# Retention, then a softplus and a squared-ReLU layer: the first chunks' loads on two queues, and three idle products ahead instead of six

## The chip, the cores and the metric

The kernel runs on one core of a Trainium2 chip. The metric is the device time of one execution in microseconds (us); the median of three timed runs stands for the kernel before. The engines are PE (TensorE, matrix products), DVE (VectorE), ACT (ScalarE), POOL (GpSimd) and SP (SyncE, which here only issues DMAs). ACT can issue DMAs too: such an instruction stands in ACT's own instruction stream, between its arithmetic.

## What is computed

A retention layer (attention with a decay in place of the softmax) of 4 sequences, 8 heads, 576 positions and 64 dimensions, and behind it two feed-forward layers over its 2304 x 512 result. All is float32.

```python
scores = scale * np.matmul(q, k.transpose(0, 1, 3, 2))
Dmat = np.where(rel >= 0, gamma[:, None, None] ** rel[None, :, :], 0.0)
attn = np.matmul(scores * Dmat, v)
x = attn.transpose(0, 2, 1, 3).reshape(2304, 512)
h = x @ w_in;   x = (np.maximum(h, 0) + np.log1p(np.exp(-np.abs(h)))) @ w_out
h = x @ w2_in;  out = np.square(np.maximum(h, 0)) @ w2_out
```

## The kernel before

The 2304 tokens are worked off in tiles of 512 and 384 tokens. The retention goes chunk by chunk (128 tokens, 8 heads, a running state), most of it woven into the steps of the first feed-forward layer. Only the four chunks of the first tile have nothing to be woven into: they are worked off ahead of everything else, in an order that is written out by hand (`with tc.manual_schedule()`), in which each engine's instructions stand in the order of the calls. This head of the program is the first 30 us, and the change is in it alone.

For each of the four chunks there are two loads. `early_qk` (L982 to L989) brings q and k with the dimensions on the partitions: four heads lie on partitions 0 to 63 (`LO`) and four on 64 to 127 (`HI`), 256 KB each, by one DMA for each half. `early_kv` (L991 to L994) brings k and v with the tokens on the partitions, 512 KB by one DMA. All of these are issued by SP, in the order of the chunks, and behind them, also by SP, the first three weight tiles (`wi_raw`, `pump_load(3)`, 512 KB each, L132) and the q, k and v of the fifth chunk (`ring`, L359). ACT issues four small loads: the table `cst` in two halves and two rows `rows_in`.

A layer below the kernel gives each DMA one of eight semaphores in turn. A DMA that takes a semaphore over waits, on the engine that issues it, until the DMA that had the semaphore before has landed. So no more than eight DMAs are under way, and which DMA waits for which follows from the order in which SP and ACT together issue them.

The engines' part of a chunk: PE makes the scores `pb` (`early_scores`, L1006), DVE multiplies them with the causal mask (`early_mask`, L1027) and v with its weights (`early_v`, L1015), PE adds to the state `st` (L1038), ACT copies it (L1044), PE makes the output `po` (L1054, L1062), DVE scales it to `x` (L1076), ACT rounds x to its upper part `xh` (L1081), and DVE makes the lower part `xl` (L1091). The scale tables in `cst` are not loaded whole: PE spreads the two rows over the partitions (`spread_rows`, L1135), ACT copies the result (L1139, L1140) and makes some of the tables by 20 small operations (L1145), DVE the others (L963). Behind the third chunk ACT begins on the first weight tile: L152 and L153 put its two words in shape, DVE joins them (L157), ACT rounds (L185), DVE takes the rest (L186), and PE can begin the first layer (`early_g1`, L1110).

Ahead of all this PE multiplies zeros (`keep_warm(6)`, L946), six products of 128 x 512 into a bank that nobody reads; one more such product stands behind `spread_rows`.

Of the kernel before, what the change touches and what calls it, by code (L numbers as in the profile page):

```python
# [45 lines left out]
def kernel(  # L46
# [26 lines left out]
    nc = tc.nc  # L73
# [203 lines left out]
    def pump_load(upto):  # L277
        while n_load[0] < min(upto, len(loads)):
            load_w(*loads[n_load[0]])
            n_load[0] += 1  # L280
# [68 lines left out]
    LO, HI = slice(0, P // 2), slice(P // 2, P)  # L349
# [5 lines left out]
    def load_chunk(c):  # L355
        if c < NPR:
            new_chunk(c)
            for i, src in ((0, qk_t), (2, kv)):
                nc.sync.dma_start(  # L359
                    out=chunk[c][:, i:i + 2],  # L360
                    in_=src[2 * c:2 * c + 2].rearrange("s p i h c -> (s p) i h c"),
                )
# [580 lines left out]
    def keep_warm(count, n=512):  # L943

        for _ in range(count):
            nc.tensor.matmul(  # L946
                cold[:, :n], lhsT=warm[:, :P], rhs=warm[:, :n], start=True, stop=True
            )
# [11 lines left out]
    def make_xw(m, n):  # L960


        nc.vector.scalar_tensor_tensor(  # L963
            out=later[:, m - 1:m - 1 + n],
            in0=cst[:, x_first].rearrange("p (a b) -> p a b", a=KD).unsqueeze(1)
            .to_broadcast([P, n, KD, CN]),
            scalar=1.0,
            in1=times[:, m - 1:m - 1 + n].unsqueeze(3).to_broadcast([P, n, KD, CN]),
            op0=ALU.mult, op1=ALU.mult,
        )  # L970
# [4 lines left out]
    qks, kvs, mixed, kept_s, pbs, pos, xs_of, kept_of = {}, {}, {}, {}, {}, {}, {}, []  # L975
    causal = first_pool.tile([P, P], F32, tag="causal", name="causal", bufs=1)

    def early_tiles(c):
        qks[c] = first_pool.tile([P, 2, 2, HH, CN], F32, tag=f"qk{c}", name="qk", bufs=1)
        kvs[c] = first_pool.tile([P, 2, H, CN], F32, tag=f"kv{c}", name="kv", bufs=1)  # L980

    def early_qk(c):  # L982
        for g, half in enumerate((LO, HI)):
            nc.sync.dma_start(
                out=qks[c][half].rearrange("p i s h c -> p i s (h c)"),
                in_=qk_t[2 * c:2 * c + 2].rearrange("s p i h c -> p i s (h c)")[
                    ..., g * HH * CN:(g + 1) * HH * CN
                ],
            )  # L989

    def early_kv(c):  # L991
        nc.sync.dma_start(
            out=kvs[c], in_=kv[2 * c:2 * c + 2].rearrange("s p i h c -> (s p) i h c")
        )  # L994

    def early_scores(c):
        if c % 2:
            pb = pbs[c] = [ps_h.tile([P, 512], F32, tag=f"h{g}", name="pb") for g in range(2)]
        else:
            pb = ps_head.tile([P, 2, 512], F32, tag="pb", name="pb", bufs=1)  # L1000
            pbs[c] = [pb]
            pb = [pb[:, g] for g in range(2)]
        for hh in range(HH):
            for s, to in enumerate((LO, HI)):
                for g, rows in enumerate((LO, HI)):
                    nc.tensor.matmul(  # L1006
                        pb[g][to, hh * P:(hh + 1) * P],
                        lhsT=qks[c][rows, 1, s, hh, :], rhs=qks[c][rows, 0, :, hh, :],
                        start=True, stop=True, skip_group_check=True,
                    )  # L1010

    def early_v(c):
        t = kvs[c][:, 1]
        w = vw[:, 2 * c * H:(2 * c + 1) * H]
        nc.vector.tensor_tensor(  # L1015
            out=t, in0=t, in1=w.unsqueeze(2).to_broadcast([P, H, D]), op=ALU.mult
        )

    def early_mask(c):
        mixed[c] = first_pool.tile([P, H, P], F32, tag="mixed", name="mixed")  # L1020
        for g, pb in enumerate(pbs[c]):
            n = H // len(pbs[c])
            if len(pbs[c]) == 1:
                pb = pb.rearrange("p g (h n) -> p (g h) n", n=P)
            else:
                pb = pb.rearrange("p (h n) -> p h n", n=P)
            nc.vector.tensor_tensor(  # L1027
                out=mixed[c][:, g * n:(g + 1) * n], in0=pb,
                in1=causal.unsqueeze(1).to_broadcast([P, n, P]), op=ALU.mult,
            )  # L1030
# [59 lines left out]
    def early_low(c):  # L1090
        nc.vector.tensor_tensor(  # L1091
            out=early_at(x_lo(), c), in0=xs_of.pop(c), in1=early_at(x_hi(), c),
            op=ALU.subtract,
        )
# [31 lines left out]
    def spread_rows():  # L1126
        rows = ps_head.tile([P, 2, 512], F32, tag="po", name="rows", bufs=1)
        to = [
            rows[:, 0, at:at + n * b].rearrange("p (a b) -> p a b", a=n)
            for at, n, b in ((0, KD, CN), (256, SCN - 1, KD))  # L1130
        ]
        for half in (LO, HI):
            one = slice(half.start, half.start + 1)
            for r, of in zip(to, (row[0][:, 0], row[0][:, 1:, :, 0])):
                nc.tensor.matmul(  # L1135
                    r[half], lhsT=ones[one], rhs=of[one],
                    start=r is to[0], stop=True, skip_group_check=True,
                )
        nc.scalar.copy(cst[:, x_first].rearrange("p (a b) -> p a b", a=KD), to[0])  # L1139
        nc.scalar.mul(times, to[1], float(D) ** 0.5)  # L1140

    def scalar_xw(m, n):
        for m in range(m, m + n):
            for a in range(KD):
                nc.scalar.activation(  # L1145
                    out=later[:, m - 1, a], in_=cst[:, C_XW + a * CN:C_XW + (a + 1) * CN],
                    func=AF.Copy, scale=times[:, m - 1, a:a + 1],
                )

    with tc.manual_schedule():  # L1150
        rows_in = xs.tile([P, SCN * KD * CN], F32, tag="xr", name="rows_in")
        for c in range(last):
            early_tiles(c)
        early_qk(0)
        for half in (LO, HI):
            nc.scalar.dma_start(out=cst[half, :C_XW], in_=consts[CN:P, :C_XW])
        early_kv(0)
        early_qk(1)
        early_kv(1)
        for r in (0, CN):  # L1160
            nc.scalar.dma_start(out=rows_in[r:r + 1], in_=consts[r:r + 1, C_XW:])
        nc.scalar.preload_act_table_set("natural_log_exp_and_others")
        for c in range(2, last):
            early_qk(c)
            early_kv(c)
        pump_load(3)
        load_chunk(last)
        nc.vector.memset(causal[LO, CN:], 1.0)
        nc.vector.memset(causal[HI, :CN], 0.0)

        for half, to, of, n in ((LO, 0, 0, SCN), (HI, 0, 1, SCN - 1), (HI, SCN - 1, 0, 1)):
            nc.vector.tensor_copy(
                vw[half, to * H:(to + n) * H], cst[half, C_VW + of * H:C_VW + (of + n) * H]
            )
        for s, half in enumerate((LO, HI)):
            nc.vector.tensor_copy(
                causal[half, s * CN:(s + 1) * CN], cst[half, C_MASK:C_MASK + CN]
            )
        keep_warm(6)
        early_scores(0)  # L1180
        row.append(rows_in.rearrange("p (m a b) -> p m a b", a=KD, b=CN))
        spread_rows()
        keep_warm(1)
        scalar_xw(4, 2)
        early_mask(0)
        early_v(0)
        make_xw(1, 1)
        early_scores(1)
        early_states(0)
        early_mask(1)  # L1190
        early_v(1)
        early_carried(0)
        early_o(0)
        early_x(0)
        early_scores(2)
        early_states(1)
        scalar_xw(6, 1)
        early_carried(1)
        early_o(1)
        make_xw(2, 2)  # L1200
        early_mask(2)
        early_v(2)
        early_x(1)
        scalar_xw(7, 2)
        early_scores(3)
        early_states(2)
        early_carried(2)
        early_o(2)
        early_low(0)
        early_mask(3)  # L1210
        early_v(3)
        begin_words()
        early_keep(0)
        early_x(2)
        next(begun[0])
        early_low(1)
        early_keep(1)
        early_states(3)
        early_carried(3)
        early_o(3)  # L1220
        next(begun[0])
        begun.clear()
        begin_words()
        early_g1(0)
        early_x(3)
        next_state(3, 1)
        begin_words()
        early_low(2)
        early_low(3)
        early_keep(2)  # L1230
        for made in begun:
            next(made)
        early_keep(3)
# [232 lines left out]
```

## Time and profile before

| | us |
|---|---|
| median of three runs | 840.74 (837.81 to 841.48) |
| span of the profiled execution | 839.0 |
| PE busy | 818.2 (98%) |
| DVE busy | 702.2 (84%) |
| ACT busy | 475.3 (57%) |
| DMA queues, mean rate | 226 GB/s |

The profiled execution's span, from its first to its last instruction, is 1.7 us below the median. PE is busy nearly throughout, so the time is the sum of PE's work and of what PE waits for. Shares over the whole span say nothing of the head, whose limits are others; for it one reads the rows in order of time. In these rows a line that issues DMAs is marked SPq or ACTq: the start is when the engine began to issue, the time what the issuing took, not the transfer. A row of several instructions shows its group's start and the whole stretch.

### The profile page before, as it was taken

The page shows a single profiled execution, that of the slowest core. Times are in us where ns is not written, and L with a number is a line of the kernel's source. Part 1 is how long each engine was busy: PE and PEld are TensorE (multiplying, and loading weights), DVE is VectorE, ACT ScalarE, POOL GpSimd, SP SyncE. Part 2 cuts the span into 40 slices and gives each one's busy share as a digit, 9 for nine tenths or more (in the row PEclk, how much of TensorE's full clock was granted, in tenths as well). Part 3 has the DMA queues.
Part 4 walks back from the last instruction along what each step waited for, and adds up shares of the span by engine and source line. Part 5 has one row for each costly group of instructions (what it writes and reads, how often), then busy time and mean ns, then how long its engine had stood idle before and what let it go on. Part 6 is the DMA issues. An engine that isn't in the chain of part 4 may idle for free.

```text
span 839.0 us, 16498 instructions
## 1 busy us (share of the span) xinstructions
PE 818.2 (98%) x5957; PEld 722.6 (86%) x5957; DVE 702.2 (84%) x1336; ACT 475.3 (57%) x899; POOL 0.2 (0%) x4
## 2 busy tenths in 40 slices
PE   8899999999999998999999999999999999999998
PEld 5677799888788876888799999988999988999887
DVE  4889887878988887787999988999698997787886
ACT  3889888757567667676888521355321554111453
POOL 0000000000000000000000000000000000000000
PEclk9999999999999999999999999999999999999999
DMA  9866544546656665466676688898988889988885
GB/s 234 298 195 235 167 141 145 176 152 214 210 174 198 224 190 176 149 227 202 210 255 219 221 253 249 259 296 275 301 257 245 255 263 280 284 254 252 254 268 176
DMA packets 122804, 189.39 MB, mean 226 GB/s; under 512 B 10466, under 2 KB 68450, under 8 KB 122722
## 3 DMA queue, kind: packets, MB, share of 16 engines
q1 hardware_dynamic: 122560, 188.26, 71.3%
q8 instruction: 47, 0.77, 0.4%
q14 instruction: 33, 0.27, 0.1%
q10 hardware_dynamic: 164, 0.09, 0.1%
HBM read 147.41 MB, written 40.89 MB: 224 GB/s over the span
## 4 chain that ended last, share of the span: by engine, by line
PE 78%; DVE 8%; ACT 8%; DMA 3%; issue 2%; SPq 0%; DVEq 0%; ACTq 0%
PE acc L563 17%; PE ph L512 16%; PE py L699 9%; PE py L772 9%; PE px L699 6%; PE pz L772 6%; PE px L772 6%; PE pz L699 6%; ACT l L527 1%; DMA wi_raw<-in_moe_w_in_dram 1%; DVE l L535 1%; DVE e L532 1%; ACT e L526 1%; ACT e L525 1%; PE po L436 1%
## 5 line engine op out<-in xcount | busy, mean ns | idle before, releaser
L512 PE MATMUL ph<-xh,wi 128*128 128x512 f32 (+1 forms) x632 | 145.1, 371 | 2.2 <-ACT l L527 1.1
L512 PEld LDWEIGHTS ph<-xh,wi 128*128 128x128 f32 x632 | 116.3, 189 | 18.7 <-issue 1.4
L563 PE MATMUL acc<-gl,woh 128*128 128x512 f32 (+1 forms) x320 | 119.0, 372 | 2.9 <-DVE gl L548 2.9
L563 PE MATMUL acc<-gh,woh 128*128 128x512 f32 (+1 forms) x320 | 120.5, 380 | 0.5 <-ACT woh L185 0.5
L563 PE MATMUL acc<-gh,wol 128*128 128x512 f32 (+1 forms) x320 | 118.7, 371 | 0.7 <-DVE wol L186 0.7
L532 DVE SCALAR_TENSOR_TENSOR e<-e 128x512 f32<-128x512 f32 (+1 forms) x80 | 51.0, 638 | 48.7 <-ACT l L527 47.8
L699 PE MATMUL py<-t,sring 128*128 128x384 f32 x432 | 88.6, 339 | 0.0
L525 ACT ACTIVATE e<-ph 128x512 f32<-128x512 f32 (+1 forms) x80 | 44.2, 553 | 60.9 <-PE ph L512 60.4
L512 PE MATMUL ph<-xl,wi 128*128 128x512 f32 (+1 forms) x316 | 77.9, 367 | 0.1
L699 PEld LDWEIGHTS py<-t,sring 128*128 128x128 f32 x432 | 74.8, 188 | 2.6 <-DVE uring L903 0.7
L563 PEld LDWEIGHTS acc<-gl,woh 128*128 128x128 f32 x320 | 60.4, 189 | 12.1 <-DVE gl L548 5.1
L752 ACT CAST gh<-g 128x384 fp32r<-128x384 f32 x84 | 43.1, 515 | 46.6 <-PE px L772 16.7
L563 PEld LDWEIGHTS acc<-gh,woh 128*128 128x128 f32 x320 | 60.4, 189 | 9.8 <-ACT woh L185 0.8
L563 PEld LDWEIGHTS acc<-gh,wol 128*128 128x128 f32 x320 | 60.5, 189 | 8.7 <-DVE wol L186 1.0
L752 ACT CAST gring<-g 128x384 fp32r<-128x384 f32 x84 | 43.1, 514 | 40.3 <-PE py L772 16.4
L512 PEld LDWEIGHTS ph<-xl,wi 128*128 128x128 f32 x316 | 58.1, 188 | 8.0 <-DVE xl L479 0.4
L899 ACT COPY uring<-px 128x384 f32<-128x384 f32 x24 | 11.5, 481 | 87.5 <-PE px L699 87.5
L699 PE MATMUL pz<-t,sring 128*128 128x384 f32 x288 | 58.4, 334 | 0.0
L699 PE MATMUL px<-t,sring 128*128 128x384 f32 x288 | 58.0, 335 | 0.0
L527 ACT ACTIVATE l<-e,cst 128x512 f32<-128x512 f32 (+1 forms) x80 | 54.4, 681 | 5.8 <-DMA x2d<-xo 3.6
L720 DVE TENSOR_TENSOR gring<-g,gring 128x384 fp32r<-128x384 f32 x84 | 46.2, 553 | 10.0 <-ACT gring L752 8.9
L720 DVE TENSOR_TENSOR gl<-g,gh 128x384 fp32r<-128x384 f32 x84 | 46.4, 554 | 9.2 <-ACT gh L752 8.0
(126 smaller groups left out, 1622.3 us busy)
## 6 DMA issues: line engine op xcount, KB each, us to landing
sring<-s2d SPq DMA_DIRECT2D x168, 256.0 KB, 3.2
sring<-o2d SPq DMA_DIRECT2D x168, 256.0 KB, 3.4
wi_raw<-in_moe_w_in_dram SPq DMA_DIRECT2D x32, 512.0 KB, 5.0
wo_raw<-in_moe_w_out_dram SPq DMA_DIRECT2D x32, 512.0 KB, 4.1
s2d<-ct SPq DMA_DIRECT2D x48, 256.0 KB, 2.7
o2d<-ct SPq DMA_DIRECT2D x48, 256.0 KB, 2.6
ring<-in_qk_t_dram SPq DMA_DIRECT2D x14, 512.0 KB, 4.8
ring<-in_kv_dram SPq DMA_DIRECT2D x14, 512.0 KB, 6.1
```

The costliest lines, as they stand in the source:

```text
L436: nc.tensor.matmul(po[(LO, HI)[hh % 2], hh // 2, :], lhsT=before[rows, hh, :] if carried else sv[:, hh, :], rhs=qp[:, hh, :] if carried el ...
L512: nc.tensor.matmul(ph[:, :n], lhsT=a, rhs=x, start=(j == 0), stop=(j == len(todo) - 1))
L525: nc.scalar.activation(out=e, in_=ph[:, :n], func=AF.Abs)
L526: nc.scalar.activation(out=e, in_=e, func=AF.Exp, scale=-1.0)
L527: nc.scalar.activation(out=l, in_=e, func=AF.Ln, bias=below_one, scale=1.0 + 2.0**-23)
L532: nc.vector.scalar_tensor_tensor(out=e, in0=e, scalar=-2.0, in1=e, op0=ALU.add, op1=ALU.mult)
L563: nc.tensor.matmul(acc[j][:, :n], lhsT=a, rhs=x, start=(begin and m == 0), stop=(end and m == 2))
L699: nc.tensor.matmul(ps, lhsT=a, rhs=x, start=(first and m == 0), stop=(m == len(todo) - 1), skip_group_check=True,)
L720: nc.vector.tensor_tensor(out=out, in0=a, in1=b, op=ALU.subtract)
L752: nc.scalar.copy(h, src)
L772: nc.tensor.matmul(blocks[m][:, :cols], lhsT=a[:, c], rhs=x, start=(first and p == n == 0), stop=(p == NP - 1 and n == len(todo) - 1), ski ...
L899: nc.scalar.copy(s1, px)
```

## The change

`early_qk` issues the lower half by SP as before and the upper half by ACT. `early_kv` issues k by SP and v by ACT, 256 KB each, where one DMA of 512 KB stood. `keep_warm(6)` becomes `keep_warm(3)`. Nothing else differs, and the orders of PE, DVE and POOL are the same but for the three products; line numbers behind L994 go up by two.

```diff
     def early_qk(c):
-        for g, half in enumerate((LO, HI)):
-            nc.sync.dma_start(
+        for g, (half, queue) in enumerate(((LO, nc.sync), (HI, nc.scalar))):
+            queue.dma_start(
                 out=qks[c][half].rearrange("p i s h c -> p i s (h c)"),
...
     def early_kv(c):
-        nc.sync.dma_start(
-            out=kvs[c], in_=kv[2 * c:2 * c + 2].rearrange("s p i h c -> (s p) i h c")
-        )
+        for i, queue in enumerate((nc.sync, nc.scalar)):
+            queue.dma_start(
+                out=kvs[c][:, i],
+                in_=kv[2 * c:2 * c + 2, :, i].rearrange("s p h c -> (s p) h c"),
+            )
...
-        keep_warm(6)
+        keep_warm(3)
         early_scores(0)
```

The first place is ACT's stream from its first instruction on. Before, four small DMAs, the load of the activation tables, and then the copy of the spread rows (DMAHW is one of the eight semaphores of DMAs; a row without brackets waits for nothing):

```order
L1156 DMA cst<-in_consts_dram 64x138 x2
L1161 DMA rows_in<-in_consts_dram 1x2304 x2
L1162 ACT_TABLE_LOAD
L1139 COPY cst<-rows 128x256 [waits PE_49]
L1140 ACTIVATE times<-rows 128x32
```

Of the change, from ACT's second instruction on:

```order
L1158 DMA cst<-in_consts_dram 64x138 x2
L993 DMA kv<-in_kv_dram 128x512
L984 DMA qk<-in_qk_t_dram 64x4x256
L993 DMA kv<-in_kv_dram 128x512 [waits DMAHW2_49]
L1163 DMA rows_in<-in_consts_dram 1x2304 [waits DMAHW3_49]
L1163 DMA rows_in<-in_consts_dram 1x2304 [waits DMAHW7_49]
L1164 ACT_TABLE_LOAD
L984 DMA qk<-in_qk_t_dram 64x4x256 [waits DMAHW3_49]
L993 DMA kv<-in_kv_dram 128x512 [waits DMAHW5_49]
L984 DMA qk<-in_qk_t_dram 64x4x256 [waits DMAHW7_49]
L993 DMA kv<-in_kv_dram 128x512 [waits DMAHW0_49]
L1141 COPY cst<-rows 128x256 [waits PE_49]
```

Eight large DMAs now stand in ACT's stream (the first of them, the upper q and k of chunk 0, just ahead of these rows), seven of ACT's DMAs have a wait, and the copy of the spread rows stands behind all of them. By the built program the last one, v of chunk 3, waits until semaphore 0 has counted three DMAs: the upper q and k of chunk 0, k of chunk 1, and the first weight tile.

The second place is the same stream at ACT's first work on that weight tile. Before:

```order
L1145 ACTIVATE cst<-cst,times 128x64 x8
L1044 COPY kept<-st 128x256 [waits PE_49,Activation_49]
L152 ACTIVATE wi_raw<-wi_raw 128x512 [waits DMAHW0_49]
L153 ACTIVATE wi_raw<-wi_raw,cst 128x512 [waits DMAHW2_49]
L1081 CAST xh<-x 128x4x128 [waits DVE_49]
```

Of the change:

```order
L1147 ACTIVATE cst<-cst,times 128x64 x8
L1046 COPY kept<-st 128x256 [waits PE_49,Activation_49]
L152 ACTIVATE wi_raw<-wi_raw 128x512
L153 ACTIVATE wi_raw<-wi_raw,cst 128x512 [waits DMAHW4_49]
L1083 CAST xh<-x 128x4x128 [waits DVE_49]
```

L152 has lost its wait for the weight tile's DMA: that wait now stands further up in ACT's stream, at the DMA of v of chunk 3.

The third place is SP's stream up to the weight tiles. Before, from the second half of chunk 2's q and k on:

```order
L984 DMA qk<-in_qk_t_dram 64x4x256 [waits DMAHW3_49]
L992 DMA kv<-in_kv_dram 128x1024 [waits DMAHW4_49]
L984 DMA qk<-in_qk_t_dram 64x4x256 [waits DMAHW5_49]
L984 DMA qk<-in_qk_t_dram 64x4x256 [waits DMAHW6_49]
L992 DMA kv<-in_kv_dram 128x1024 [waits DMAHW7_49]
L132 DMA wi_raw<-in_moe_w_in_dram 128x4x256 [waits DMAHW0_49]
```

Of the change, from k of chunk 1 on:

```order
L993 DMA kv<-in_kv_dram 128x512 [waits DMAHW0_49]
L984 DMA qk<-in_qk_t_dram 64x4x256 [waits DMAHW1_49]
L993 DMA kv<-in_kv_dram 128x512 [waits DMAHW4_49]
L984 DMA qk<-in_qk_t_dram 64x4x256 [waits DMAHW5_49]
L993 DMA kv<-in_kv_dram 128x512 [waits DMAHW6_49]
L132 DMA wi_raw<-in_moe_w_in_dram 128x4x256 [waits DMAHW0_49]
```

On SP eight DMAs of 256 KB stand ahead of the first weight tile where it was twelve of 256 and 512 KB; that tile's DMA waits for k of chunk 1, where it waited for the upper q and k of chunk 1.

## Rows read from the trace of the kernel before

**Rows 1.** The page's first line.
```profile
span 839.0 us, 16498 instructions
```

**Rows 2.** Chain of waits, head: start, time, what.
```profile
11.28 11.36 DMA wi_raw<-in_moe_w_in_dram
```

**Rows 3.** Timeline of ACT: start, stretch, instructions, idle time ahead and its cause.
```profile
1.97 1.03 ACTq L1161 DMA_DIRECT2D rows_in<-in_consts_dram  x2
3.03 1.28 ACT L1162 ACT_TABLE_LOAD   x1 [3.03 <-issue]
10.81 0.37 ACT L1139 COPY cst<-rows 128x256 f32<-128x256 f32 x1 [6.50 <-PE rows L1135]
11.32 2.02 ACT L1145 ACTIVATE cst<-cst,times 128x64 f32<-128x64 f32 x8
13.51 0.37 ACT L1044 COPY kept<-st 128x256 f32<-128x256 f32 x1 [0.17 <-PE st L1038]
15.42 0.62 ACT L1081 CAST xh<-x 128x512 fp32r<-128x512 f32 x1 [1.54 <-DVE x L1076]
17.39 1.06 ACT L1145 ACTIVATE cst<-cst,times 128x64 f32<-128x64 f32 x4
22.66 0.68 ACT L152 ACTIVATE wi_raw<-wi_raw 128x512 f32<-128x512 f32 x1 [0.40 <-DMA wi_raw<-in_moe_w_in_dram]
```

**Rows 4.** Windows: busy time by engine, granted clock (1.00 is full), DMA share, GB/s.
```profile
0.00:2.90 2.90, 1.45 (x2) 0.84 (x3) 0.74 (x4) 0.00 (x0) 0.20 (x4) 1.00 0.25 19
2.90:11.26 8.36, 8.36 (x53) 3.80 (x51) 1.98 (x6) 1.73 (x3) 0.00 (x0) 1.00 1.08 265
11.26:15.34 4.08, 3.44 (x68) 2.37 (x66) 3.47 (x8) 2.42 (x10) 0.00 (x0) 1.00 1.10 255
15.34:19.27 3.93, 3.70 (x81) 2.87 (x81) 2.99 (x5) 1.95 (x6) 0.00 (x0) 1.00 1.09 253
19.27:22.64 3.37, 3.03 (x72) 2.38 (x74) 2.42 (x5) 2.80 (x10) 0.00 (x0) 1.00 1.09 353
33.00:36.40 3.40, 3.40 (x10) 2.70 (x9) 3.19 (x6) 1.15 (x2) 0.00 (x0) 0.52 1.02 404
```

**Rows 5.** Timeline of DVE, same columns as the timeline of ACT.
```profile
11.87 0.42 DVE L963 SCALAR_TENSOR_TENSOR cst<-cst,times 128x256 f32<-128x256 f32 x1
12.90 1.29 DVE L1027 TENSOR_TENSOR mixed<-pb,causal 128x512 f32<-128x512 f32 x2 [0.61 <-PE pb L1006]
14.10 0.68 DVE L1015 TENSOR_TENSOR kv<-kv,vw 128x512 f32<-128x512 f32 x1
14.70 0.68 DVE L1076 TENSOR_TENSOR x<-po,cst 128x512 f32<-128x512 f32 x1
15.30 0.68 DVE L963 SCALAR_TENSOR_TENSOR cst<-cst,times 128x512 f32<-128x512 f32 x1
16.52 1.23 DVE L1027 TENSOR_TENSOR mixed<-pb,causal 128x1024 f32<-128x1024 f32 x1 [0.54 <-PE pb L1006]
```

**Rows 6.** Who waited for whom on SP's queue, first 30 us: total, times, longest.
```profile
SPq L132 <- DMA kv<-in_kv_dram: 1.4, 1, 1.4
```

**Rows 7.** Timeline of PE, same columns.
```profile
1.45 7.58 PE L946 MATMUL cold<-warm 128*128 128x512 f32 x12 [1.45 <-DVE warm L940]
32.38 0.68 PE L388 MATMUL pb<-ring 64*64 64x64 f32 x16 [2.65 <-DVE ring L398]
32.99 3.67 PE L512 MATMUL ph<-xh,wi 128*128 128x512 f32 x8
39.76 2.09 PE L512 MATMUL ph<-xh,wi 128*128 128x512 f32 x8 [1.07 <-ACT l L527]
```

## The prediction

> **What bounds the kernel now.** Over the whole span PE is at work for 98% of 839.0 us [rows 1], so anything that shifts the head of the program shifts the end; nothing later is tied to the clock on the wall. The chain of waits says what sets the head: the first weight tile is issued at 11.28 and lands 11.36 later, at 22.64 [rows 2], and ACT's first operation on it, L152, starts at 22.66 after an idle time of 0.40 for that DMA [rows 3]. That is the number to watch: from L152 on, ACT and DVE hand the weight tiles to one another with no other wait for a load, and PE's first layer follows. Next read the timeline of ACT: it waits 6.50 for the spread rows, starts its copy at 10.81, and has from there to 22.66, 11.85 us, for its part of the first chunks [rows 3]. So two things must be ready for L152: the tile, and ACT itself. ACT is ready only 0.40 before the tile; it has no more slack than that. Third, the windows: from 2.9 to 19.27 the queues move 265, 255 and 253 GB/s, then 353 [rows 4]. The edges 11.26, 15.34 and 19.27 are about where the upper q and k of chunks 1, 2 and 3 land, so each of the second and third windows holds one chunk, 1.05 MB in 4 us. The slow windows hold the loads that fill only 64 partitions each; the fast one holds loads over all 128.
>
> **The change part by part.**
>
> *The halves at once.* What the split can bring is the rate. At 353 GB/s a chunk would take 3.0 us instead of 4.0, about 4 us over four chunks. The first tile then lands earlier; by how much comes next.
>
> *When the first weight tile lands.* Ahead of it on SP's queue are eight pieces of 262,144 bytes, 2.10 MB, and itself 0.52: 2.62 MB. On ACT's queue, moved beside them, are the upper halves and v of chunks 0 and 1 (1.05 MB), the tables (0.09) and the upper q and k of chunk 2 (0.26), 1.40 MB, and at most 0.5 of the later pieces, which wait for others. I take 4.1 MB in all, with the two queues sharing alike (an estimate; before, ACT's queue held next to nothing). Before, the windows give 5.49 MB moved by 22.64 [rows 4], while q, k, v, the tables and the tile are 4.80; so a landing is seen some 0.69/0.353 = 2.0 us after its last byte. With a start at 2.7 (2.9 less what had moved by then) the tile lands at 2.7 + 4.1/0.353 + 2.0 = 16.3 at the fast rate and at 2.7 + 4.1/0.26 + 2.0 = 20.5 at the slow one. I take the middle, 18.4: halves run side by side only while both queues have work, and ACT's runs dry whenever its next issue waits.
>
> *ACT's stream.* This is the cost. A DMA that waits holds back everything behind it on its engine: SP shows it, its weight-tile issue waited 1.4 us for a kv load [rows 6]. ACT now has eight large DMAs ahead of its first copy, and the last, v of chunk 3, waits for semaphore 0, that is for the first weight tile to have landed. L152 has even lost its own wait for it. So ACT's copy, at 10.81 before, starts at 18.4 plus that last issue, 0.5 (half of the 1.03 for two [rows 3]): 18.9. Queued behind it: the copy of the spread rows, all of ACT's table operations, the copies of the state, the casts. Waiting for these: DVE's L963 and with it the mask of chunk 1, and PE's first output, whose bank the spread rows still hold.
>
> *How long ACT then needs to L152.* All loads but the last v's have landed or land before their turn, so DVE's waits of 0.61 and 0.54 for scores [rows 5] and most of ACT's 1.54 for x [rows 3] go. Counted from ACT's copy: at 0.5 the rows are spread (11.32 - 10.81 [rows 3]); DVE does table, masks, v and x of chunk 0, 0.42 + 1.29 + 0.68 + 0.68, with some 0.08 of overlap at each seam (14.10 against 12.90 + 1.29 [rows 5]), to 3.4; then tables, mask 1.23, v and x of chunk 1, 0.68 three times, to 6.3. ACT's own work up to there, 2.02 + 0.37 + 0.62 + 0.37 + 1.06 [rows 3], is 4.4 and hidden. Behind x of chunk 1 ACT casts (0.62), makes eight tables (2.02), copies the state (0.37): 9.3. Before it was 11.85, so the waits for loads that go are worth 2.5 us. L152 starts at 18.9 + 9.3 = 28.2 instead of 22.66: **5.5 us later**. With 9.3 to go, ACT's copy would have to start by 22.66 - 9.3 = 13.4 for nothing to change.
>
> *Three idle products fewer.* The six take 7.58 us as twelve passes and end at 9.03 [rows 7]; three end near 6, and the scores of chunk 0 can start once q and k are there. That gains nothing: PE's next work needs `rows_in`, which ACT issued at 1.97 before [rows 3] and now issues only after the upper q and k of chunk 1 have landed. PE is idle there for some 5 us. [...] Here PE mostly waits for DVE, so the price lies between 0 and 1.6; I take 0.4, nearer to the cover. It cannot be below nothing, since fewer products make PE no warmer. ACT's table load (1.28 [rows 3]) lies in the idle time.
>
> *The sum.* 5.5 + 0.4 = 5.9 us. The span would go from 839.0 to 844.9, and the median, which lies 1.7 above the span, from 840.74 to **846.6**. The bounds: the tile at 16.3 gives 3.4, the tile at 20.5 gives 7.6 and with 1.6 for the clock 9.2: 844.1 to 850.0.
>
> **The rivals.**
>
> *The load rate decides, and ACT is not held (faster).* If v of chunk 3 were issued early, ACT could copy as soon as the rows are spread, and the tile would land at 16.3 to 18.4. ACT's 9.3 us from a copy at 10.81 reach L152 at 20.1, 2.5 us sooner: 838.2. It turns from loss to gain where ACT's copy starts before 13.4. For it: the windows at 255 GB/s. Against it: the order of ACT's stream, and `rows_in` itself, which now lands late. A gain above 0.5%, 4.2 us, would need the copy at 9.2, before the rows can be there. Chance 0.08.
>
> *The halves do not run side by side (slower still).* Both queues then move the 260 GB/s of the head [rows 4], the tile lands at 20.5, and without the clock the loss is 7.6: 848.3. For it: each half alone was slow. Against it: the tile's own loads reach 353 with the same size of piece. Chance 0.2.
> [...]
>
> *The delay is small or is taken up (no change).* The tile lands at or before 16.3, and DVE finds some of its later waits gone, or part of the shift falls into PE's idle 2.65 us at 32.38 [rows 7]. Against the last: that wait is for DVE, which is late by as much. It would give 0 to 4 us, 843 as its middle. Chance 0.22.
>
> **How the numbers follow.** The forecast itself, ACT held until the tile has landed in between, has the chance 0.5 and the time 846.6. What a measurement of this kernel can tell from no change is about 0.5%, 4.2 us, so slower begins at 844.9. The forecast lies above that for 0.47 of its 0.5, and the serialized halves lie there wholly, 0.2: 0.67, and 0.01 from the third rival. Faster by 0.5% is left 0.05, for the first rival and what both mechanisms miss; the rest is within. The range reaches up to 850.0, the bound of both costs, and down to 842.5, which takes in the upper half of the no-change case.
>
> **What the profile would show.** ACT's row of L1141 (L1139 before) starts at 17 to 21 instead of 10.81, right behind an ACTq row of v; L152 starts at 26.5 to 30.5, with no wait for its DMA; DVE has a gap of 5 us or more ahead of L963; PE has one ahead of the spread rows; ACT's queue moves some 2.2 MB instead of 0.09. If the halves run side by side, the windows between 3 and 11 show more than 300 GB/s. The forecast is wrong if ACT copies before 13.4, and its size is wrong if the stretch from that copy to L152 is far from 9.3.

## The result, and the profile of the changed kernel

The changed kernel takes 849.01 us (median of six runs, 846.85 to 851.1) against 840.65 for the kernel before (six runs, 837.81 to 841.48): a ratio of 1.0102, with a 95% interval of 1.0085 to 1.012. It is slower, by twice what a measurement of this kernel can tell from no change, and within the forecast's range, 1.0 us below its upper end and 2.4 us above its centre. The profiled execution took 847.9 us, 1.1 us less than the median; its span is 7.0 us longer than [rows 1]. The page's first line, and its rows of the two DMA queues (packets, MB, share), q1 being SP's and q10 ACT's:

```profile
span 846.0 us, 16489 instructions
q1 hardware_dynamic: 121472, 186.16, 69.3%
q10 hardware_dynamic: 1828, 2.19, 1.0%
```

ACT's timeline, from the load of the spread rows to the first work on a weight tile (start, stretch, instructions, idle time ahead and its cause):

```profile
6.43 3.98 ACTq L1163 DMA_DIRECT2D rows_in<-in_consts_dram  x2
10.44 1.28 ACT L1164 ACT_TABLE_LOAD   x1 [10.44 <-DMA qk<-in_qk_t_dram]
...
18.34 0.36 ACTq L993 DMA_DIRECT2D kv<-in_kv_dram  x1
18.74 0.37 ACT L1141 COPY cst<-rows 128x256 f32<-128x256 f32 x1 [7.02 <-DMA qk<-in_qk_t_dram]
...
23.92 0.62 ACT L1083 CAST xh<-x 128x512 fp32r<-128x512 f32 x1 [1.44 <-DVE x L1078]
...
26.98 0.62 ACT L1083 CAST xh<-x 128x512 fp32r<-128x512 f32 x1 [1.01 <-DVE x L1078]
...
29.68 0.68 ACT L152 ACTIVATE wi_raw<-wi_raw 128x512 f32<-128x512 f32 x1
```

The copy that stood at 10.81 [rows 3] stands at 18.74, right behind the issue of v of chunk 3. L152 has moved from 22.66 to 29.68, by 7.0 us, as much as the span, and no longer waits for its tile. When that tile lands is told by the row of its issue, in the view of the DMAs between 10.7 and 11.3 (the last figure is the time to landing); it was issued at 10.79, so it landed at 18.3, just where v's issue stands:

```profile
wi_raw<-in_moe_w_in_dram SPq DMA_DIRECT2D x1, 512.0 KB, 7.5
```

The bracket behind ACT's copy names a load of q and k, not the tile: it gives what ended most of an idle time in which ACT issued four DMAs. That the last of these waited for the tile is told by the built program and by the two times, 18.3 and 18.34; in two kernels below with the same order of DMAs (x4 and x5) the same row names the tile.

DVE's timeline has the gap, 9.6 us ahead of L963, and a second, short one ahead of the mask of chunk 1:

```profile
19.25 0.43 DVE L963 SCALAR_TENSOR_TENSOR cst<-cst,times 128x256 f32<-128x256 f32 x1 [9.59 <-ACT times L1142]
21.40 1.29 DVE L1029 TENSOR_TENSOR mixed<-pb,causal 128x512 f32<-128x512 f32 x2 [1.72 <-PE pb L1008]
```

PE's timeline says where that second gap comes from:

```profile
5.69 1.10 PE L1008 MATMUL pb<-qk 64*64 64x128 f32 x32
12.94 1.24 PE L1137 MATMUL rows<-rows_in,ones 1*64 1x256 f32 x4 [6.15 <-DMA rows_in<-in_consts_dram]
16.16 1.27 PE L1137 MATMUL rows<-rows_in,ones 1*64 1x256 f32 x4 [1.97 <-DMA rows_in<-in_consts_dram]
17.36 2.08 PE L946 MATMUL cold<-warm 128*128 128x512 f32 x2
19.36 1.99 PE L1008 MATMUL pb<-qk 64*64 64x128 f32 x32
```

The scores of chunk 0 took 1.10 and those of chunk 1, the same 32 products, 1.99. The windows (length, busy time of PE, its weight loads, DVE, ACT and POOL, granted clock, DMA share, GB/s) have the clock at 0.50 from 12 to 21:

```profile
2.90:11.26 8.36, 3.90 (x37) 1.73 (x35) 2.76 (x7) 0.82 (x1) 0.00 (x0) 1.00 1.09 260
11.26:15.34 4.08, 1.24 (x4) 0.73 (x4) 0.00 (x0) 0.46 (x1) 0.00 (x0) 0.50 1.09 255
12.00:21.00 9.00, 6.09 (x42) 3.56 (x42) 0.43 (x1) 2.23 (x10) 0.00 (x0) 0.50 1.09 297
```

Their last column is the change's whole purpose, and it has not moved: 260 and 255 GB/s where [rows 4] has 265 and 255. What the two queues did at the start is told by their rows apart. First from 2.0 to 3.2, then from 3.2 to 4.5 (packets, MB, share of the stretch):

```profile
q10 hardware_dynamic: 245, 0.25, 59.7%
q1 hardware_dynamic: 4, 0.00, 1.0%
```

```profile
q1 hardware_dynamic: 267, 0.26, 96.1%
q10 hardware_dynamic: 72, 0.04, 17.0%
```

One upper half (0.25 MB), then one lower half (0.26 MB): the halves of chunk 0 were issued at once, both at 0.73, and moved one after the other. Later the queues did share: from 5.6 to 6.2 SP's has 63.4% and ACT's 40.5%, and the rate there is 320 GB/s, from 6.2 to 7.5 it is 44.4%, 69.5% and 191. Last, the chain of waits in the head (start, time, what):

```profile
3.43 6.73 DMA qk<-in_qk_t_dram
10.18 5.93 DMA rows_in<-in_consts_dram
16.16 1.27 PE rows L1137 x4
17.43 2.00 PE cold L946 x2
19.43 1.92 PE pb L1008 x32
```

It goes through a wait for the upper q and k of chunk 1, the second spread row behind it, and PE at half clock: not through the weight tile. So two delays end within a few us of one another, ACT's hold at 18.7 and PE's late scores at 21.4. It is the second that ends last: DVE was done with L963, which needs ACT, at 19.68 and waited until 21.40 for the scores. The experiments have to tell what each is worth. Both come from the same place, DMA issues in ACT's stream that wait: the second spread row was issued at 10.18, right behind the landing in the chain's first row.

### The profile page after: what moved, and what is told of

It is laid out like the page before. It is cut to its first block, busy times and chain, and to the rows that moved or that the text cites. A ratio compares the mean times of both kernels' runs of the same rounds, so it can differ in the third digit from the quotient of the medians.

```text
span 846.0 us, 16489 instructions
## 1 busy us (share of the span) xinstructions
PE 817.9 (97%) x5951; PEld 724.4 (86%) x5951; DVE 702.3 (83%) x1336; ACT 474.9 (56%) x899; POOL 0.2 (0%) x4
## 3 DMA queue, kind: packets, MB, share of 16 engines
q10 hardware_dynamic: 1828, 2.19, 1.0%
## 4 chain that ended last, share of the span: by engine, by line
PE 82%; DVE 7%; ACT 7%; DMA 2%; issue 2%; ACTq 0%; DVEq 0%
PE acc L563 19%; PE ph L512 18%; PE py L699 9%; PE py L772 9%; PE px L699 6%; PE pz L772 6%; PE px L772 6%; PE pz L699 6%; PE po L436 1%; ACT l L527 1%; DVE xl L479 1%; DVE l L535 1%; DVE e L532 1%; ACT e L526 1%; ACT e L525 1%
## 5 line engine op out<-in xcount | busy, mean ns | idle before, releaser
L512 PEld LDWEIGHTS ph<-xh,wi 128*128 128x128 f32 x632 | 116.5, 190 | 18.3 <-issue 1.4
L752 ACT CAST gh<-g 128x384 fp32r<-128x384 f32 x84 | 43.2, 516 | 46.2 <-PE px L772 16.1
L720 DVE TENSOR_TENSOR g<-g 128x384 f32<-128x384 f32 x96 | 52.6, 554 | 1.5
```

The lines of the kernel that those rows point to most:

```text
L512: nc.tensor.matmul(ph[:, :n], lhsT=a, rhs=x, start=(j == 0), stop=(j == len(todo) - 1))
L720: nc.vector.tensor_tensor(out=out, in0=a, in1=b, op=ALU.subtract)
L752: nc.scalar.copy(h, src)
```

## The experiments

The theory (A): ACT's arithmetic is held behind its DMA issues, the last of which waits for the weight tile. Rivals: (B) the spread rows, landing late, hold PE and so ACT; (C) the clock, or the three products fewer; (D) the load rate, with the halves moved one after the other. x4 and x5 issue their DMAs in the order of the changed kernel, and still ACT's copy comes 0.6 to 0.7 us later in them: a difference of that size between two profiles tells nothing by itself. The table has for each kernel the median, the ratio with its 95% interval, and the starts of ACT's copy of the spread rows and of L152 (L153 in x8 and x12) in its profiled execution. L152's shift follows the change of the median within some 2 us in all of them, so the head is indeed where the time is decided.

| kernel | median | ratio (95%) | copy | L152 |
|---|---|---|---|---|
| before | 840.65 | | 10.81 | 22.66 |
| changed | 849.01 | 1.0102 (1.0085 to 1.012) | 18.74 | 29.68 |
| x11_hold_only | 850.92 | 1.0128 (1.0108 to 1.0149) | 22.85 | 32.69 |
| x2_act_free | 848.87 | 1.0103 (1.0067 to 1.0138) | 18.03 | 30.13 |
| x3_rows_early | 851.39 | 1.0123 (1.0092 to 1.0154) | 20.36 | 32.62 |
| x1_rows_early_act_free | 844.71 | 1.005 (1.0029 to 1.0071) | 11.83 | 27.94 |
| x4_warm_mid | 851.09 | 1.0108 (1.007 to 1.0147) | 19.41 | 31.25 |
| x5_six | 849.31 | 1.0107 (1.0084 to 1.013) | 19.33 | 31.56 |
| x6_three_alone | 840.67 | 0.9999 (0.9982 to 1.0016) | 9.99 | 22.88 |
| x9_qk_only | 844.72 | 1.0043 (1.0024 to 1.0061) | 14.00 | 27.16 |
| x10_kv_only | 843.44 | 1.0021 (1.0 to 1.0041) | 12.11 | 24.47 |
| x7_all_partitions_1k | 840.38 | 0.9993 (0.9978 to 1.0009) | 11.40 | 21.67 |
| x8_one_dma | 838.72 | 0.9979 (0.9962 to 0.9995) | 11.54 | 21.81 |
| x12_one_dma_three | 836.61 | 0.9948 (0.9928 to 0.9969) | 8.88 | 19.17 |

**The hold by itself.** Before, with one small DMA on ACT that reads the first weight tile and stands ahead of the copy; no load is changed.

```diff
+        held = dram.tile([1, 16], U32, name="held")
+        nc.scalar.dma_start(out=held, in_=staged["wi", 0][:1, :16, 0])
```

> The kernel before with one DMA added: ACT copies 64 bytes of the first weight tile to DRAM, issued ahead of its copy of the spread rows. It waits for the tile to land, so ACT is held until then as in the changed kernel, and no load is changed. If holding ACT is a loss by itself, its copy starts at 22.7 to 23.2 us instead of 10.81, L152 9.3 to 10.9 later, at 32 to 34 instead of 22.66, and the time is 850 to 852. If ACT's part can be made up, the time is 840 to 843.

Measured 850.92, as theory A has it. ACT's timeline has nothing but the wait in it:

```profile
22.24 0.56 ACTq L1168 DMA_DIRECT2D held<-wi_raw  x1
22.85 0.37 ACT L1139 COPY cst<-rows 128x256 f32<-128x256 f32 x1 [18.51 <-DMA wi_raw<-in_moe_w_in_dram]
...
32.69 0.69 ACT L152 ACTIVATE wi_raw<-wi_raw 128x512 f32<-128x512 f32 x1
```

One waiting DMA issue in ACT's stream costs 10.8 us here (0.0128 of 840.6) without touching a load, the idle products or the rows. The mechanism is enough for a loss of this size. But its hold ends at 22.85, 4.1 us later than in the changed kernel, because the tile lands later here. From the copy to L152 it takes 9.84 us; with that stretch a copy at 18.74 would have L152 at 28.6, 5.9 later than before, where the changed kernel's is 7.0 later.

**ACT free, the rows as late.** The changed kernel, with v of chunk 3 issued by SP, so that no DMA of ACT's waits for the weight tile.

```diff
-        for i, queue in enumerate((nc.sync, nc.scalar)):
+        for i, queue in enumerate((nc.sync, nc.sync if c == 3 else nc.scalar)):
```

> The changed kernel with v of chunk 3 issued by SP. ACT's last DMA then waits for the rows, not for the weight tile; the rows still land late. If ACT's wait for the weight tile (its copy at 18.74 us) is what ends last, as the prediction has it, the copy comes at 17.5 and the time falls by 1.2 to about 847.8. If the late rows end last, by way of PE (rows at 16.16, the idle product and the scores of chunk 1 behind them, mask of chunk 1 at 21.40), the mask stays at 21.4 and the time at 848.5 to 849.5.

Measured 848.87, as the changed kernel; four runs do not tell this from the 847.8 of the other branch (the interval reaches from 846 to 852), so it is the trace that decides. ACT's copy comes at 18.03 with its cause now the PE, L152 at 30.13; the chain is that of the changed kernel, half a us later:

```profile
10.73 5.96 DMA rows_in<-in_consts_dram
16.73 1.27 PE rows L1137 x4
18.00 2.00 PE cold L946 x2
20.00 1.90 PE pb L1008 x32
```

So B holds too: the late rows alone bring L152 to where the changed kernel has it. In the changed kernel the two holds end side by side, and to lift the one that ends first gains nothing.

**The rows early.** The same (v of chunk 3 by SP), with `rows_in` issued ahead of the upper q and k of chunk 1. ACT's last DMA (the upper q and k of chunk 3) still waits for the weight tile.

```diff
+        for r in (0, CN):
+            nc.scalar.dma_start(out=rows_in[r:r + 1], in_=consts[r:r + 1, C_XW:])
         early_qk(1)
         early_kv(1)
-        for r in (0, CN):
-            nc.scalar.dma_start(out=rows_in[r:r + 1], in_=consts[r:r + 1, C_XW:])
```

> The changed kernel with rows_in issued by ACT ahead of the upper q and k of chunk 1, and v of chunk 3 by SP. By the semaphores that result ACT's last DMA still waits for the first weight tile, while the rows land early. If ACT's wait for the tile is enough for the loss, ACT copies at 18.5 to 19.5 us as before, L152 starts 9.3 later, at 28 to 29, and the time is 847 to 848.5. If the late rows are the whole loss, the time falls to 840 to 842.

Measured 851.39. The rows are spread by 12.8 and yet ACT copies at 20.36; the chain goes through the tile, and then through the load that was issued behind that wait:

```profile
10.66 9.02 DMA wi_raw<-in_moe_w_in_dram
19.70 9.74 DMA qk<-in_qk_t_dram
29.48 1.72 PE pb L1008 x30
```

With the rows out of the way A alone keeps ACT until 20.4. But the loss is larger than the copy's place explains: what waits behind the tile is here a load that PE needs, and it lands 9.74 us after its late issue.

**Both away.** The changed kernel, with `rows_in` issued by SP right behind the lower q and k of chunk 0, not by ACT. ACT's DMAs then wait for earlier ones, none for the tile.

```diff
         early_qk(0)
+        for r in (0, CN):
+            nc.sync.dma_start(out=rows_in[r:r + 1], in_=consts[r:r + 1, C_XW:])
...
-        for r in (0, CN):
-            nc.scalar.dma_start(out=rows_in[r:r + 1], in_=consts[r:r + 1, C_XW:])
```

> The changed kernel with one edit: the two DMAs of rows_in are issued by SP right behind the lower q and k of chunk 0. All eight large DMAs stay on ACT's queue and the three products stay three. By this edit the semaphores also fall out otherwise: the last DMA on ACT, v of chunk 3, now waits for the upper q and k of chunk 1 and no longer for the first weight tile. Theory: the loss is ACT's stream, held by two waits that the change put into it (the rows issued and landed late, at 16.1 us, and ACT's copy behind the weight tile, at 18.7). Then ACT copies at 9 to 12 us, L152 starts when the tile is there, 20 to 23 us, and the time is 839 to 843. Rival 1, the three products fewer leave PE cold and that is the loss: 847 to 849. Rival 2, loads on two queues run slower: the tile lands later than 22.6 us, 843 to 846.

Measured 844.71, half of the loss; the expectation of no loss did not hold. ACT's copy is at 11.83, so the hold is gone. PE's timeline has a new wait, and SP's tells its cause:

```profile
16.81 1.98 PE L1008 MATMUL pb<-qk 64*64 64x128 f32 x32 [3.01 <-DMA qk<-in_qk_t_dram]
```

```profile
1.53 3.51 SPq L1158 DMA_DIRECT2D rows_in<-in_consts_dram  x2
6.30 0.35 SPq L993 DMA_DIRECT2D kv<-in_kv_dram  x1
7.82 0.63 SPq L984 DMA_DIRECT2D qk<-in_qk_t_dram  x1
```

The rows stand in SP's stream until 5.04, and its next issues wait too: the lower q and k of chunk 1 are issued at 7.82 (the changed kernel: 2.42), by the chain right behind the landing of ACT's v of chunk 0 at 7.80, and land at 16.8. By then ACT had issued its loads for chunks 2 and 3. Here SP's issue stood behind a landing of ACT's, so this kernel moved the hold from ACT to SP.

**The clock.** The changed kernel with ten idle products between the scores of chunk 0 and the spread rows.

```diff
         early_scores(0)
+        keep_warm(10)
```

> The changed kernel with ten more idle products between the scores of chunk 0 and the spread rows, where PE is idle from 6.8 to 12.9 and from 14.2 to 16.1 us; no DMA is touched. If the granted clock of 0.50 from 12 to 21.5 us is what makes the stretch from ACT's copy to L152 10.9 instead of the 9.3 that was forecast, PE does the rows' second half, the idle product and the scores of chunk 1 in 2.8 us instead of 5.2, the mask of chunk 1 starts at 19.7 instead of 21.4, and the time is 847.0 to 847.8. If the stretch is long for another reason it stays 849.

Measured 851.09; the interval of its four runs, 846.3 to 852.8, takes in both branches, so again the trace has to tell. The first half went as expected: the clock is full from 16.7 to 22.0, the scores of chunk 1 take 1.10, and from ACT's copy to its cast of the second x it is 6.67 us, where the changed kernel has 8.24 (18.74 to 26.98):

```profile
19.41 0.37 ACT L1141 COPY cst<-rows 128x256 f32<-128x256 f32 x1 [6.67 <-DMA wi_raw<-in_moe_w_in_dram]
26.08 0.62 ACT L1083 CAST xh<-x 128x512 fp32r<-128x512 f32 x1 [1.02 <-DVE x L1078]
```

The clock is worth 1.6 us up to there. What came after took it back. PE's timeline, from the second spread row on:

```profile
17.69 0.75 PE L1137 MATMUL rows<-rows_in,ones 1*64 1x256 f32 x4 [0.26 <-DMA rows_in<-in_consts_dram]
...
19.43 1.10 PE L1008 MATMUL pb<-qk 64*64 64x128 f32 x32
...
27.84 1.98 PE L1008 MATMUL pb<-qk 64*64 64x128 f32 x30 [2.18 <-DMA qk<-in_qk_t_dram]
```

The upper q and k of chunk 3, issued at 17.67, land 10.13 us later. In the changed kernel that half is issued at 16.13, and its products start at 26.13 without a wait. So a third delay stands close behind the other two, and what the clock is worth in the median this run does not say.

**The three products.** The changed kernel with six again (x5), and the kernel before with three (x6, the opposite edit).

```diff
-        keep_warm(3)
+        keep_warm(6)
```

> The whole change with six idle products instead of three. The DMAs wait as in the changed kernel, so ACT's copy stays at 18 to 19 us and, if that is the loss, the time at 848 to 850. If the three products are part of it (PE's granted clock of 0.50 from 12 us on), the clock falls some 3 us later, the scores of chunk 1 run at full speed and the time is 847 or less.

> The kernel before with three idle products ahead instead of six, its loads untouched. If the three products matter only by where they end, PE makes the scores of chunk 0 at 6.6 us instead of 8.96, ACT copies the rows some 2 us earlier, and L152 still waits for the first weight tile at 22.6: 840 to 841. If the loss of the change is a colder PE, the granted clock falls in the gap ahead of the scores of chunk 1 and the time is 843 or more.

Measured 849.31 and 840.67. Six do not save the clock, which is 0.50 from 15.34 to 22.64 in x5; three cost the kernel before nothing, although its clock is 0.73 between 9.0 and 15.3. C falls, as far as the products go; the half clock itself is part of the chain of the changed kernel.

**One half of the change each.** x9: q and k by two queues, k and v by one DMA as before. x10: k and v by two queues, q and k by SP. Both with three products. The edits to the changed kernel:

```diff
-        for i, queue in enumerate((nc.sync, nc.scalar)):
-            queue.dma_start(
-                out=kvs[c][:, i],
...
+        nc.sync.dma_start(
+            out=kvs[c], in_=kv[2 * c:2 * c + 2].rearrange("s p i h c -> (s p) i h c")
+        )
```

```diff
-        for g, (half, queue) in enumerate(((LO, nc.sync), (HI, nc.scalar))):
+        for g, (half, queue) in enumerate(((LO, nc.sync), (HI, nc.sync))):
```

> Half of the change: q and k on two queues, k and v in one DMA on SP, three products. ACT's last DMA, the upper q and k of chunk 3, now waits for k and v of chunk 1, which land at about 10 us, and the rows wait only for a table. If the loss is ACT's held stream, ACT copies at 11 to 13 us, L152 starts when the tile is there, and the time is 840 to 842.5. If two queues for the halves lose by themselves, the time is 844 or more. If they gain, the windows up to 19 us show over 300 GB/s and the time is below 839.

> The other half of the change: k on SP, v on ACT, q and k on SP as before, three products. ACT's last DMA, v of chunk 3, waits for the lower q and k of chunk 1, at about 10 us. If the loss is ACT's held stream, ACT copies at 11 to 13 us and the time is 840 to 842.5. If splitting k and v loses by itself (v of chunk 0 and 1 is moved ahead of q and k), it is 844 or more.

Measured 844.72 and 843.44. Both lie above the 842.5 that the theory allowed, x9 in the branch of two queues that lose by themselves, x10 between the two branches with an interval that reaches down to no loss. With four large DMAs on ACT its copy stands at 14.00 and 12.11, later than before, and no DMA of ACT's waits for the tile; the loss is less than half in either. So there are losses that the wait for the tile does not make. The chains tell them; first x9, then x10:

```profile
10.48 9.83 DMA qk<-in_qk_t_dram
20.36 1.10 PE pb L1006 x30
```

```profile
5.26 5.49 DMA rows_in<-in_consts_dram
14.08 1.92 PE pb L1008 x32
```

In x9 the upper q and k of chunk 2 are issued by ACT only at 10.48, behind another landing (before, by SP between 5.4 and 7.0), and PE gets them at 20.36. In x10 it is the second spread row that is issued late and lands late, and the scores of chunk 1 run at half clock (1.99 us, from 14.01; granted 0.50 from 11.26 to 15.34): delay B without the hold. Neither gains from its split: 265, 244 and 251 GB/s in the first three windows of x9, 261, 234 and 251 in x10. The losses by the ratios, 3.6 and 1.8, sum to 5.4 of 8.6; that the rest needs both parts of the change is just clear of the intervals, and that it is the wait for the tile is not shown.

**The slow loads.** Is it the partitions or the small pieces? The kernel before, with q and k of each of the first four chunks by one DMA to all 128 partitions, in pieces of 1 KB (x7), or of 4 KB a partition from values that lie ready in that order in memory (x8; putting them in that order is not part of the measured time).

```diff
+            out=qks[c].rearrange("p i s h c -> p (i s) (h c)"),
+            in_=qk_t[2 * c:2 * c + 2].rearrange("s p i (g h) c -> (s p i g) (h c)", g=2)
+            .rearrange("(a p) x -> p a x", p=P),
```

```diff
+            out=qks[c], in_=qk0[c].rearrange("p (i s h c) -> p i s h c", i=2, s=2, c=CN)
```

> The kernel before, but q and k of each of the first four chunks come by one DMA of 512 KB to all 128 partitions, in pieces of 1 KB as before; the values land in other places, so the first chunks' scores are not the reference's. If it is the 64 partitions of a half that make the head's loads slow, the windows up to 19 us show 330 to 350 GB/s instead of 255, the tile lands at 18.5 to 19.5 instead of 22.64, and the time is 837 to 839. If it is the pieces of 1 KB, the rate stays at 255 GB/s and the time at 840 to 841.

> The kernel before with the q and k of the first four chunks laid out in DRAM as the tile wants them, so that one DMA of 512 KB brings 4 KB to each of the 128 partitions; the values are right. It loads what the change wanted to load at once, by one queue. Expected the same rate as all partitions in pieces of 1 KB if partitions are the cause: tile at 18.5 to 19.5 us, L152 at 20 to 21, bound by ACT's own part, and 837 to 839. If the rate in the head has another cause: 840 to 841.

Measured 840.38 and 838.72. The rate of the first window is 374 and 387 GB/s where it was 265 [rows 4], with pieces of 1 KB almost as with 4. The window of x7:

```profile
2.90:11.26 8.36, 8.36 (x51) 3.80 (x49) 1.39 (x6) 1.28 (x1) 0.00 (x0) 1.00 1.06 374
```

So it is not the pieces; what is left is the 64 partitions. Both kernels also make one DMA of 512 KB out of two of 256, and the size of a DMA was not tried apart from the partitions; x10, which halves the DMAs of k and v and leaves them on 128 partitions, speaks against it with 261 for 265. The faster loads bring little, since the chain of x7 (and of x8, with 8.31) begins with what the loads used to hide:

```profile
1.45 8.17 PE cold L946 x12
```

**Both limits.** x8 with three idle products.

```diff
-        keep_warm(6)
+        keep_warm(3)
```

> The kernel with q and k of a chunk in one DMA of 128 partitions (its head moved 366 to 398 GB/s, but its chain of waits began with the six idle products, which end at 9.7 us), with three products. If ACT's copy and not the tile is now what ends last, the copy comes at 8 us instead of 11.5, L152 at 17.5 to 19 instead of 21.8, and the time is 835.5 to 837.5. If something else ends last in the head it stays at 838.7.

Measured 836.61, 0.52% less than before and the fastest of all. Its window and ACT's copy:

```profile
2.90:11.26 8.36, 8.36 (x91) 4.33 (x91) 3.32 (x9) 3.63 (x11) 0.00 (x0) 1.00 1.02 392
```

```profile
8.88 0.37 ACT L1136 COPY cst<-rows 128x256 f32<-128x256 f32 x1 [4.70 <-PE rows L1132]
```

The three products, worth nothing in x6 and x5, are worth some 2 us here (838.72 to 836.61; L152 comes 2.64 earlier), where the loads no longer end last. DVE still waits for PE in it, 1.17 ahead of the mask of chunk 1, since the scores stand behind the spread rows and an idle product, and its chain still begins with the three products (5.06).

## Why the prediction was right, step by step

**ACT's stream: right as a cost, but not the path that ended last.** The copy was put at 18.9 and stands at 18.74; the wait stands where it was said to; L152 has no wait for its tile; ACT's queue moves 2.19 MB (2.2 were named). x11 shows that such a wait is by itself enough for a loss of this size, with a hold that ends 4.1 us later. But a second hold, the rows that land at 16.1, was seen in the prediction as idle time of PE and not as a hold of its own: "all loads but the last v's have landed or land before their turn" did not hold. By the chain of the changed kernel the rows are what ends last, 1.7 us behind ACT's hold, and x2, without the wait for the tile, is as slow. The wait for the tile alone would have made L152 about 5.3 us late (18.74 and 9.2, against 22.66). So the cause, ACT's waiting DMA issues, was right; that the one named ends so near the one that decided is luck.

**When the tile lands: right by two errors.** 18.4 was forecast, 18.3 measured. The rate was taken between 260 and 353; it is 263 from 2.7 to 18.34. And 2.0 us were added between a tile's last byte and its landing. From 2.7, 4.1 MB at 0.263 MB a us without that tail gives 18.3: the one error made up for the other. The 0.69 MB from which the tail was worked out can as well be bytes of the two further tiles, which SP had issued by 15.06. "The two queues sharing alike" failed for the first 2.5 us, as the two rows of the queues show.

**The rival of the halves that do not run side by side: its mechanism came true, not its sum.** Its tile was due at 20.5, its time 848.3; the time is near, 849.0, but for other reasons. That the halves of chunk 0 did not run side by side is in the trace: 260 GB/s in the first window, and from 2.0 to 3.2 us 245 packets of ACT's queue, 0.25 MB, against 4 of SP's, whose 0.26 MB followed. That a half alone is slow agrees with x7: 374 GB/s in the first window with all 128 partitions, against 265 with halves in the same pieces.

**From the copy to L152: right, but for the clock.** 9.3 was forecast and 10.94 measured, of which DVE's wait of 1.72 for the scores of chunk 1 is the difference; without it 9.2 remain.

**The clock: the term that was mis-sized.** Out of 0 to 1.6, 0.4 was taken, "nearer to the cover". The 1.6 is what eight products took longer before, at a granted clock of 0.52 [rows 4]: 3.67 against 2.09 [rows 7]; the 0.4 was the author's estimate, and no run shows it. It cost 1.7, just above its bound; x4 shows 1.6 for it directly. It could cost that much only because the rows were late. The rows landed at 16.16, and from there spread rows, idle product and scores took 1.27 + 2.00 + 1.92 = 5.2 us by the chain; in x4, at the full clock, the same three took 2.84 (17.69 to 20.53). At that speed the scores would have been there at 19.0, ahead of DVE's L963, which ends at 19.68, and nobody would have waited. The cover, DVE's own work, was gone in this one place, because DVE had been idle for 9.6 us and had nothing left to do ahead of the mask.

**The sum.** 5.5 + 0.4 = 5.9 was forecast for the span: 0.16 less for the copy, 0.1 less for the rest of the stretch and 1.3 more for the clock give 6.9 to 7.0, the shift of L152 and of the span. The medians differ by 8.4; the profiled span of 846.0 lies below the middle of the six executions' spans (844.7 to 848.3, the middle 846.8), so 0.8 of the other 1.4 is the choice of the execution.

**No change and the gain.** Neither came. x1, the nearest to "ACT not held", is still 4.2 us slower, so the gain of that rival needed the rate as well, which two queues did not give (260 GB/s in the first window). Break-even was put at a copy at 13.4; x10, with 12.11, is already slower, by 1.8 (at the edge of its interval), and its L152 as much later (24.47), because a copy that follows the spread rows at once finds the scores not there yet (DVE waits 3.00 for them in x10): the stretch is then 10.3 at the full clock (x7, x8 and x12) and 12.36 in x10, with 0.50 from 11.26 to 15.34 and 0.85 from there to 19.27.

**What stays open.** Why the two queues' halves are moved one after the other, and why a half of 256 KB takes 9 to 10 us to land from ACT's queue (x3, x4) among SP's loads. That 64 partitions and not the size of a DMA make the slow loads is argued. How the loss divides between the hold and the late rows is open too: each alone ends within 2 us of the other, and no kernel had the late rows with neither the hold nor the half clock.

## What to carry to other kernels

A DMA issued from an engine that also computes is an instruction in that engine's stream (behind the one of x11 ACT's copy stood at 22.85, not at 10.81): before moving one there, find out which landing its issue waits for, and count everything queued behind it. Two transfers to the two halves of the partitions gained nothing here by two queues (260 GB/s in the first window, 265 before); one transfer that fills all 128 partitions did raise the rate (374 in x7, 387 in x8), and then what the slow load used to hide (here the idle products) has to be cut as well (838.72 to 836.61 us). Where several waits ended close together, taking one away showed nothing (x2, 848.87 for 849.01): an experiment that adds the one suspected wait to the old kernel says more.

## What the runs showed of the hardware that was not expected

- At the start two queues were served nearly one DMA at a time: from 2.0 to 3.2 us 245 packets of ACT's against 4 of SP's, although SP had issued its half at the same 0.73.
- A load of 9 KB (`rows_in`), issued among 256 KB ones, took 5.93 us to land; in x4 6.46.
- In the changed kernel PE's work ended at 6.8 and the granted clock was full until 11, 0.64 in the next us, and 0.50 until 21, though PE was busy for 6.1 of the 9 us from 12 on.
- The rate of the first window went from 265 to 374 GB/s, with q and k in the same 1 KB pieces, when each of their DMAs filled 128 partitions instead of 64.
